# Fused attention and MLP-mixer on one core: the first batch's mask, score tiles and value products regrouped, and its loads issued ahead of the constants

## The chip, the cores and the metric

The kernel runs on 1 core of one Trainium2 chip. The metric is the device time of one execution in microseconds (us); lower is better. Engines are named as in the profile: PE (TensorE matmul), PEld (TensorE weight load), DVE (VectorE), ACT (ScalarE), POOL (GpSimd), SP (SyncE, which here only starts transfers).

## The reference, cut to what matters

```
q, k, v: (8 batches, 8 heads, 576 positions, 64), s: (8, 8, 576)
scores = q @ k^T / 8                        # per batch and head
cum    = cumsum(max(s, 0))
scores = causal ? -1e9 : scores + min(-(cum_i - cum_j), 0)
attn   = softmax(scores)
x      = concat over heads (attn @ v)       # (8, 576, 512)
h      = relu(x^T @ w_tok1) @ w_tok2        # token mixing, 576 -> 256 -> 576
u      = x + h^T
out    = u + relu(u @ w_ch1) @ w_ch2        # channel mixing, 512 -> 1536 -> 512
```

The kernel folds the bias into v: row j of v, and a column of ones beside it, is multiplied by a weight made from exp(cum_j). The product with exp(scores) then gives numerator and denominator together. Only the block diagonal and the block before it are computed (for query block ic, the key blocks ic-1 and ic). A flag, summed at the end, sends the program to a slow general version where this does not hold; with the given inputs it does hold.

## The kernel before, in words

All work is recorded as operations in a `Plan` (helper class at the top). Each operation has an estimated cost per engine that may run it, the things it reads and writes, the ring buffers it holds, and a priority. `Plan.run` is a greedy list scheduler: it puts each operation at its earliest estimated time and so writes a fixed order for each engine. Each engine then runs its list in that order, and a semaphore holds an instruction until what it reads is there. The planner knows nothing of two engines that slow each other, and it fills planned PE gaps in the first 95 us with dummy matmuls on zeros (L947, "fill"), so a PE wait early in the run shows partly as fills. Changing any cost, priority or buffer therefore moves the order of all five lists.

Per batch b (0 to 7) there are four stages.

1. Loads. `stage_qk` (L573) brings k and q of a group of four heads into a `qkn` tile by POOL transfers (L563); a square sum for the flag (L569, ACT) reads the same tiles. `stage_v` (L525) brings v in five chunks of 128 rows (L534: POOL transfers for b = 0 and 1, SP transfers from b = 2), and five multiplies per batch write the weighted copy `vp` (L546; on DVE or POOL for b = 0, on POOL alone after that). The ones column is written by L555 and L557 on POOL. There are two `vf` tiles and two `vp` tiles, one for even and one for odd batches. Eight POOL transfers can be open at a time: a POOL transfer waits for the landing of the eighth before it.
2. Attention. `quad` (L586) turns k and q of four heads with two DVE transposes (L591, into `kT` and `qT`), computes scores on PE (L620) in two column groups (gi = 0 and 1) for two pairs of heads (e = 0 and 1), each into a two-bank PSUM tile `psc` (ring of 2, L415). `soft` takes exp on ACT (L639, 1024 columns) into a ring of four `E` tiles and, for b > 0, multiplies the diagonal blocks by a triangle `keep` on DVE (L647 and L655: the two masks of gi = 1, one of gi = 0). For b = 0 the mask is added on PE instead: an identity matmul of `negm` (L615) ahead of each 128-wide diagonal piece, and the scores are cut into 128-wide pieces to match. `pair` multiplies with `vp` (L677, 9 matmuls a head into one bank `pav`), takes the reciprocal (L684) and writes normalised heads to `x` (L689), one head at a time.
3. Token mixing, `tok` (L724). L742 multiplies x with w_tok1 (two PSUM banks from the ring `pmx`, 3 banks), a relu gives `h` (L752 on ACT or L753 on DVE), L763 multiplies with w_tok2, and the sum with x is made by L766 and L777 (b = 0, PE and ACT) or by a DVE add (L773, into `ub`, `ua` or the shared `us`). The result is transposed: by PE (L799) and a copy (L807, L809) for b = 0 and 1, by an SP transfer (L790) after that.
4. Channel mixing, `chan` (L813). L827 multiplies with w_ch1, L834 (ACT) or L836 (DVE) takes the relu, L845 multiplies with w_ch2, L856 adds and the output leaves by SP (L861, L864).

The order of the weight loads is written by hand at the end (L867 on): after k, q and v of batch 0 come w_tok1 and w_tok2, the four parts of w_ch1, k, q and v of batch 1, and the three parts of w_ch2 (all L699, POOL). A tiny SP transfer (L880, `gate`) waits for the last of these, and the SP loads of v for batch 2 stand behind it.

The start: POOL builds the identity matrices, `keep` and `negm`, and then issues the first loads. The weights `wT` come from s by a chain of ACT, DVE and PE (L484 to L503).

Of the kernel before, what the change touches and what calls it, by code (L numbers as in the profile page):

```python
# [337 lines left out]
def kernel(  # L338
# [12 lines left out]
    nc = tc.nc  # L351
# [30 lines left out]
    negm = sb("negm", [128, 128], BF16, fast)  # L382
# [22 lines left out]
    r_rc = ring("rc", 4, [128, NJ], FP32)  # L405
# [11 lines left out]
    r_mx = ring("pmx", 3, [128, 512], FP32, psum)  # L417
# [14 lines left out]
    nc.vector.memset(zero[:, :], 0.0)  # L432

    def consts():
# [3 lines left out]
    P.op({"POOL": (1.3, 1.5, consts)}, writes=["const"], prio=0)  # L438
    P.op({"POOL": (0.25, 0.45, lambda: nc.gpsimd.tensor_scalar(
        out=negm[:, :], in0=keep[:, :], scalar1=30000.0, scalar2=-30000.0, op0=ALU.mult, op1=ALU.add))},  # L440
        reads=["const"], writes=["negm"], prio=0)
# [38 lines left out]
    def act(n, fn, bias=False):  # L480
# [7 lines left out]
        reads=["sr"], writes=["cum"], prio=-1)  # L488
    P.op(dve(1, lambda: nc.vector.tensor_scalar(
        out=half[:, :], in0=cum[:, S - 1 : S], scalar1=-0.5, scalar2=None, op0=ALU.mult)),  # L490
        reads=["cum"], writes=["half"], prio=-1)
# [3 lines left out]
    bw = Buf(r_mx, False)  # L495

    def w_tr():
        for jc in range(NJ + 1):
            j0 = jc * 128 if jc < NJ else S - 128
            nc.tensor.transpose(out=bw.t[:, jc * 64 : jc * 64 + 64], in_=wn[:, j0 : j0 + 128],  # L500
                                identity=identf[:, :])
    P.op({"PE": (0.7, 1.1, w_tr)}, reads=["wn", "const"], writes=[(bw, 0)], prio=(0,))
    P.op(dve(384, lambda: nc.vector.tensor_copy(  # L503
        out=wT[:, :, :].rearrange("p c e -> p (c e)"), in_=bw.t[:, 0:384])),
        reads=[(bw, 0)], writes=["wT"], prio=-1)
# [17 lines left out]
    vbuf = {}  # L523

    def stage_v(b):  # L525
# [14 lines left out]
        for c in range(NJ):  # L540
# [11 lines left out]
            P.op(alts, reads=[(vf, c), "wT"], writes=[(vp, c)], prio=b * 10 + 5 if b else 0)  # L552
# [32 lines left out]

    def quad(b, qd):  # L586
# [11 lines left out]
        for gi, group in enumerate(([(0, 0, 256), (1, 128, 384)], [(2, 256, 512), (3, 384, 576), (4, 512, 576)])):  # L598
            pss = [Buf(r_sc, False) for e in range(2)]
# [6 lines left out]
            def mm(heads, pss=pss, cols=cols):  # L606
                for (jc, a, z, c0) in cols:
                    j0 = S - 128 if odd and jc == NJ - 1 else jc * 128
                    cuts = sorted({a, min(z, a + 128), z}) if b == 0 else [a, z]
                    for a1, z1 in zip(cuts, cuts[1:]):  # L610
                        o = slice(c0 + a1 - a, c0 + z1 - a)
                        masked = b == 0 and a1 == a
                        if masked:
                            for g in heads:
                                nc.tensor.matmul(out=pss[g // 2].t[:, g % 2, o], lhsT=ident[:, :], rhs=negm[:, 0 : z1 - a1],  # L615
                                                 start=True, stop=False)
                        for e in range(2):
                            for g in heads:
                                rows = slice(32 * g, 32 * g + 32)
                                nc.tensor.matmul(out=pss[g // 2].t[:, g % 2, o], lhsT=kT.t[rows, j0 : j0 + 128, e],  # L620
                                                 rhs=qT.t[rows, a1:z1, e], start=(e == 0 and not masked), stop=(e == 1))
            if b == 0:
                for e in range(2):
                    P.op({"PE": (0.9, 1.2, lambda e=e, mm=mm: mm((2 * e, 2 * e + 1)))},
                         reads=[(kT, 0), (qT, 0), "negm"] + ([("pad", np_ + e)] if 0 < np_ + e < 4 else []),
                         writes=[(pss[e], 0)], holds=[Es[e]], prio=(np_ + e, 1))
            else:
                P.op({"PE": (0.65, 0.95, lambda mm=mm: mm((0, 1, 2, 3)))}, reads=[(kT, 0), (qT, 0)],
                     writes=[(pss[0], 0), (pss[1], 0)], holds=Es, prio=(np_, 1))
            for e in range(2):  # L630
                soft(b, gi, group, pss[e], Es[e])
        for e in range(2):
            pair(b, qd, e, Es[e])

    def soft(b, gi, group, ps, E):
# [4 lines left out]
        P.op(act(1024, ex), reads=[(ps, 0)], writes=[(E, jc) for (jc, a, z) in group], prio=0)  # L640
# [18 lines left out]
    def pair(b, qd, e, E):  # L659
# [8 lines left out]
        for hh in range(2):  # L668
            pa, rc = Buf(r_mx if b == 0 and hh else r_av, False), Buf(r_rc, False)

            def av(pa=pa, hh=hh):
                o = pa.t[:, 0 : NJ * 66].rearrange("p (c n) -> p c n", n=66)
                for ic in range(NJ):
                    j_lo = max(ic - 1, 0)
                    for jc in range(j_lo, ic + 1):
                        d0 = ewin(jc, ic, odd)
                        nc.tensor.matmul(out=o[:, ic, 0 : D + 1], lhsT=E.t[:, hh, d0 : d0 + 128],  # L677
                                         rhs=vp.t[:, jc, h + hh, 0 : D + 1], start=(jc == j_lo), stop=(jc == ic))
            P.op({"PE": (9 * 0.031, 9 * 0.031 + 0.3, av)}, reads=ekeys + vkeys, writes=[(pa, 0)],
                 holds=[x, rc], prio=(np_, 0))  # L680

            def rcp(pa=pa, rc=rc):
                o = pa.t[:, 0 : NJ * 66].rearrange("p (c n) -> p c n", n=66)
                nc.vector.reciprocal(out=rc.t[:, :], in_=o[:, :, D])  # L684
            P.op(dve(30, rcp), reads=[(pa, 0)], writes=[(rc, 0)], prio=0)

            def nrm(pa=pa, rc=rc, hh=hh):
                o = pa.t[:, 0 : NJ * 66].rearrange("p (c n) -> p c n", n=66)
                nc.vector.tensor_tensor(  # L689
                    out=x.t[:, :, (h + hh) * D : (h + hh + 1) * D], in0=o[:, :, 0:D],  # L690
                    in1=rc.t[:, :].unsqueeze(2).to_broadcast([128, NJ, D]), op=ALU.mult)
            P.op(dve(330, nrm), reads=[(pa, 0), (rc, 0)], writes=[(x, h + hh)], prio=0)
# [25 lines left out]
    gate = sb("gate", [1, 16], BF16, fast)  # L718
# [5 lines left out]
    def tok(b):  # L724
# [11 lines left out]
        heads = [(0, 4), (4, 6), (6, H)] if b == 0 else [(0, H)]  # L736
        pms = [Buf(r_mx, False) for t in range(NTC)]
        for (ha, hb) in heads:
            for t in range(NTC):
                def mm(t=t, pm=pms[t], ha=ha, hb=hb):  # L740
                    for c in range(NJ):
                        nc.tensor.matmul(out=pm.t[:, ha * D : hb * D],  # L742
                                         lhsT=w1[:, NJ if odd and c == NJ - 1 else c, t * 128 : t * 128 + 128],
                                         rhs=x.t[:, c, ha * D : hb * D], start=(c == 0), stop=(c == NJ - 1))
                occ = 5 * c_pe((hb - ha) * D)[0]
                P.op({"PE": (occ, occ + 0.3, mm)},
                     reads=[(x, hh) for hh in range(ha, hb)] + ["w1", "padw"],
                     writes=[(pms[t], ha)], holds=[h1], prio=(rank - TOK, 0))
        for t in range(NTC):
            pm = pms[t]  # L750
            P.op(either(512,
# [244 lines left out]
```

## Time and profile before

| what | value |
|---|---|
| three runs | 314.44, 317.94, 314.12 us; median 314.44 |
| profiled execution, its own time | 317.43 us |
| its span in the trace | 315.6 us (1.8 us lie around it) |
| busy in the span | PE 291.2, PEld 166.1, DVE 186.4, ACT 169.8, POOL 80.3 us |
| fills (L947) | 16.0 us of PE's busy time, 7.0 of it before 9.35 us |
| mean clock granted to PE | 0.976 |
| chain that ended last | PE 76%, DVE 11%, DMA 5%, issue 3%, POOL 3% of the span |

The profile cuts the span into 40 slices of 7.9 us and gives the busy tenths of each engine, the clock granted to PE in tenths, and the busy share of the 16 DMA engines. The waits name for each engine what ended its idle time. The timeline lists instructions with start and duration. A line such as L827 is a line of the kernel before.

### The profile page before, as it was taken

The page shows a single profiled execution, that of the slowest core. Times are in us where ns is not written, and L with a number is a line of the kernel's source. Part 1 is how long each engine was busy: PE and PEld are TensorE (multiplying, and loading weights), DVE is VectorE, ACT ScalarE, POOL GpSimd, SP SyncE. Part 2 cuts the span into 40 slices and gives each one's busy share as a digit, 9 for nine tenths or more (in the row PEclk, how much of TensorE's full clock was granted, in tenths as well). Part 3 has the DMA queues.
Part 4 walks back from the last instruction along what each step waited for, and adds up shares of the span by engine and source line. Part 5 has one row for each costly group of instructions (what it writes and reads, how often), then busy time and mean ns, then how long its engine had stood idle before and what let it go on. Part 6 is the DMA issues. An engine that isn't in the chain of part 4 may idle for free.

```text
span 315.6 us, 6588 instructions
## 1 busy us (share of the span) xinstructions
PE 291.2 (92%) x2632; PEld 166.1 (53%) x2663; DVE 186.4 (59%) x391; ACT 169.8 (54%) x274; POOL 80.3 (25%) x123
## 2 busy tenths in 40 slices
PE   7989989992999998999999999996999999999991
PEld 3566875541676544454774545553764545447540
DVE  6843596999599678455744857694615534350020
ACT  3453965883499367621684268873773256107400
POOL 8764660197015212500160101740000000000000
PEclk9999999997599999999999999998999999999999
DMA  5999999999945896916421854499002410051032
GB/s 107 224 206 232 200 210 217 198 258 245 193 77 117 161 134 134 216 40 120 98 39 39 132 140 75 97 139 209 0 2 51 117 66 3 35 122 63 1 105 73
DMA packets 58343, 38.65 MB, mean 122 GB/s; under 512 B 44480, under 2 KB 47936, under 8 KB 58304
## 3 DMA queue, kind: packets, MB, share of 16 engines
q0 software_dynamic: 10128, 17.93, 33.6%
q1 hardware_dynamic: 48176, 20.21, 27.2%
q8 instruction: 23, 0.38, 0.5%
q14 instruction: 16, 0.13, 0.1%
HBM read 40.71 MB, written 9.44 MB: 159 GB/s over the span
## 4 chain that ended last, share of the span: by engine, by line
PE 76%; DVE 11%; DMA 5%; issue 3%; POOL 3%; ACT 0%; SPq 0%; POOLq 0%; DVEq 0%
PE pmx L827 28%; PE pmx L845 26%; PE psc L620 6%; PE pmx L742 5%; PE pav L677 5%; PE pmx L763 4%; DMA uTb<-ub 3%; DVE ub L773 2%; DVE E L647 2%; POOL vp L546 2%; DVE qT L591 2%; DVE kT L591 2%; DVE x L689 2%; DMA qkn<-in_k_dram 1%; PE psc L615 1%
## 5 line engine op out<-in xcount | busy, mean ns | idle before, releaser
L639 ACT ACTIVATE E<-psc 128x1024 bf16<-128x1024 f32 x64 | 62.5, 1024 | 36.6 <-PE psc L620 36.4
L827 PEld LDWEIGHTS <-wc 128*128 128x128 bf16 x624 | 59.6, 99 | 37.0 <-issue 6.1
L827 PE MATMUL pmx<-uTb,wc 128*128 128x320 bf16 x384 | 59.4, 309 | 3.3 <-DMA uTb<-ub 3.1
L845 PE MATMUL pmx<-wc,gb 128*128 128x512 bf16 x231 | 54.0, 379 | 0.5 <-issue 0.2
L834 ACT ACTIVATE gb<-pmx 128x320 bf16<-128x320 f32 x74 | 32.2, 439 | 29.3 <-PE pmx L827 24.3
L569 ACT ACTIVATE junk<-qkn 128x1152 bf16<-128x1152 bf16 x32 | 37.4, 1169 | 14.5 <-DMA qkn<-in_k_dram 8.8
L845 PE MATMUL pmx<-wc,ga 128*128 128x512 bf16 x184 | 44.2, 379 | 0.7 <-DVE ub L773 0.2
L827 PE MATMUL pmx<-uTa,wc 128*128 128x512 bf16 (+1 forms) x237 | 44.4, 336 | 0.2
L546 POOL TENSOR_TENSOR vp<-vf,wT 128x512 bf16<-128x512 f32 (+1 forms) x35 | 37.2, 1082 | 7.5 <-issue 5.1
L845 PEld LDWEIGHTS <-gb 128*128 128x128 bf16 x240 | 22.5, 98 | 25.4 <-issue 0.4
L563 POOL DMA_DIRECT2D qkn<-in_k_dram x20 | 11.2, 562 | 94.0 <-DVE gb L836 22.9
L677 PEld LDWEIGHTS <-E 128*128 128x128 bf16 x576 | 25.7, 98 | 13.5 <-issue 3.7
L834 ACT ACTIVATE ga<-pmx 128x512 bf16<-128x512 f32 (+1 forms) x43 | 21.8, 508 | 20.4 <-PE pmx L827 19.7
L647 DVE TENSOR_TENSOR E<-E,keep 128x512 bf16<-128x512 bf16 x56 | 28.4, 511 | 4.4 <-ACT E L639 4.4
L689 DVE TENSOR_TENSOR x<-pav,rc 128x320 bf16<-128x320 f32 x60 | 29.4, 490 | 1.8
L677 PE MATMUL pav<-vp,E 128*128 128x65 bf16 x540 | 26.7, 194 | 3.7 <-DVE x L689 2.4
L845 PEld LDWEIGHTS <-ga 128*128 128x128 bf16 x192 | 17.7, 98 | 19.8 <-issue 0.7
L684 DVE RECIPROCAL rc<-pav 128x5 f32<-128x5 f32 x60 | 11.2, 187 | 28.3 <-PE pav L677 28.0
L620 PE MATMUL psc<-qT,kT 32*128 32x256 bf16 (+3 forms) x704 | 25.4, 246 | 0.5 <-DVE qT L591 0.2
L763 PE MATMUL pmx<-h,w 128*128 128x512 bf16 x77 | 20.7, 380 | 2.7 <-DVE ub L773 2.6
L591 DVE STREAM_TRANSPOSE kT<-qkn 128x576 f32<-128x576 f32 x16 | 20.0, 1251 | 4.8 <-PE psc L620 3.3
L856 DVE TENSOR_TENSOR of<-pmx,us 128x512 f32<-128x512 f32 x4 | 2.8, 692 | 33.0 <-PE pmx L845 25.1
(84 smaller groups left out, 262.6 us busy)
## 6 DMA issues: line engine op xcount, KB each, us to landing
out_dram<-of SPq DMA_DIRECT2D x32, 256.0 KB, 2.8
vf<-in_v_dram SPq DMA_DIRECT2D x24, 256.0 KB, 5.4
qkn<-in_k_dram POOLq DMA_DIRECT2D x20, 288.0 KB, 5.5
qkn<-in_q_dram POOLq DMA_DIRECT2D x20, 288.0 KB, 6.5
vf<-in_v_dram POOLq DMA_DIRECT2D x8, 256.0 KB, 9.9
wc<-in_moe_w_ch_dram POOLq DMA_DIRECT2D x4, 384.0 KB, 8.8
wc<-in_moe_w_ch_dram POOLq DMA_DIRECT2D x3, 512.0 KB, 11.6
out_dram<-of SPq DMA_DIRECT2D x8, 128.0 KB, 2.4
```

The lines of the kernel that those rows point to most:

```text
L546: eng.tensor_tensor(out=vp.t[p0 : p0 + n, c, :, 0:D], in0=vf.t[p0 : p0 + n, c, :, :], in1=wT[p0 : p0 + n, cw, b * H : b * H + H].unsqueeze ...
L569: P.op({"ACT": (1.2, 1.6, lambda: nc.scalar.activation(out=junk[:, :], in_=n.t[:, :], func=AF.Square, accum_out=sq[:, col : col + 1]))}, r ...
L591: P.op({"DVE": (1.24, 1.4, lambda n=n, dst=dst: nc.vector.transpose(out=dst.t[:, 0:S, :].rearrange("d t e -> d (t e)").bitcast(FP32).rearr ...
L620: nc.tensor.matmul(out=pss[g // 2].t[:, g % 2, o], lhsT=kT.t[rows, j0 : j0 + 128, e], rhs=qT.t[rows, a1:z1, e], start=(e == 0 and not mask ...
L639: nc.scalar.activation(out=E.t[:, :, gi * 512 : gi * 512 + 512], in_=ps.t[:, :, :], func=AF.Exp, scale=0.125)
L647: nc.vector.tensor_tensor(out=o, in0=o, in1=keep[:, :].unsqueeze(1).unsqueeze(1).to_broadcast([128, 2, 2, 128]), op=ALU.mult)
L677: nc.tensor.matmul(out=o[:, ic, 0 : D + 1], lhsT=E.t[:, hh, d0 : d0 + 128], rhs=vp.t[:, jc, h + hh, 0 : D + 1], start=(jc == j_lo), stop=( ...
L689: nc.vector.tensor_tensor(out=x.t[:, :, (h + hh) * D : (h + hh + 1) * D], in0=o[:, :, 0:D], in1=rc.t[:, :].unsqueeze(2).to_broadcast([128, ...
L763: nc.tensor.matmul(out=pm.t[:, :], lhsT=w2[:, t, w0 : w0 + 128], rhs=h1.t[:, t, :], start=(t == 0), stop=(t == NTC - 1 and b > 0))
L827: nc.tensor.matmul(out=pm.t[:, 0 : e - a], lhsT=wc1[:, m, cc * 128 : cc * 128 + 128], rhs=uT.t[:, m, a:e], start=(m == 0), stop=(m == NMC ...
L834: lambda cc=cc, pm=pm, a=a, e=e: nc.scalar.activation(out=g.t[:, cc, a:e], in_=pm.t[:, 0 : e - a], func=AF.Relu),
L845: nc.tensor.matmul(out=pm.t[:, :], lhsT=g.t[:, cc, c * 128 : c * 128 + 128], rhs=wc2[:, cc, :], start=(cc == 0), stop=(cc == NCC - 1))
```

## The change

The first batch is regrouped, and some orders are moved.

- `negm` grows from 128 to 512 columns: zero except three triangles, at columns 0, 256 and 448. For b = 0 one 512-wide identity matmul per head and column group writes the whole bank of mask, and the score matmuls are no longer cut: 256, 192 and 64 columns wide, as for the other batches.
- The three `pmx` banks become one tile, and a `Duo` of two free banks of it serves as a third score tile for b = 0 (two of the eight score tiles).
- For b = 0 the products of two heads go into one two-bank `psc` tile, with one reciprocal and one normalisation per pair.
- The first four loads of k and q are issued on POOL ahead of the constants; the constants and `wT` follow them. `wT` may be copied by ACT.
- `tok` is split by heads for b = 0 (heads 0 to 3 in two `pmx` banks; 4 to 7 in one `psc` tile) and for b = 1 (heads 0 to 3, then 4 to 7).
- The PE transposes of `tok` get a priority between its matmuls, and stores of the output a lower one than other SP work.
- A POOL operation copies one element of each of batch 1's last two `E` tiles into `gate` and is recorded as the writer of "m1", which batch 2's five `vp` multiplies are recorded as reading. Those five are recorded earlier than the writer.

```
-    negm = sb("negm", [128, 128], BF16, fast)
+    negm = sb("negm", [128, 512], BF16, fast)
...
-    r_rc = ring("rc", 4, [128, NJ], FP32)
+    r_rc = ring("rc", 4, [128, 2, NJ], FP32)
...
-    r_mx = ring("pmx", 3, [128, 512], FP32, psum)
+    mxt = psum.tile([128, 3, 512], FP32, name="pmx", tag="pmx")
+    r_mx = Ring("pmx", [mxt[:, i, :] for i in range(3)])
...
+    nc.vector.memset(negm[:, :], 0.0)
...
-    P.op({"POOL": (1.3, 1.5, consts)}, writes=["const"], prio=0)
-    P.op({"POOL": (0.25, 0.45, lambda: nc.gpsimd.tensor_scalar(
-        out=negm[:, :], in0=keep[:, :], scalar1=30000.0, scalar2=-30000.0, op0=ALU.mult, op1=ALU.add))},
-        reads=["const"], writes=["negm"], prio=0)
+    def negs():
+        for a, w in ((0, 128), (256, 128), (448, 64)):
+            nc.gpsimd.tensor_scalar(out=negm[:, a : a + w], in0=keep[:, 0:w], scalar1=30000.0, scalar2=-30000.0,
+                                    op0=ALU.mult, op1=ALU.add)
+    def load_consts():
+        lastp[0] = P.op({"POOL": (1.3, 1.5, consts)}, writes=["const"], prio=0, after=lastp[0])
+        lastp[0] = P.op({"POOL": (0.7, 0.9, negs)}, reads=["const"], writes=["negm"], prio=0, after=lastp[0])
...
-            P.op(alts, reads=[(vf, c), "wT"], writes=[(vp, c)], prio=b * 10 + 5 if b else 0)
+            P.op(alts, reads=[(vf, c), "wT"] + (["m1"] if b == 2 else []), writes=[(vp, c)], prio=b * 10 + 5 if b else 0)
...
+    class Duo:
+        def __init__(self):
+            self.bufs = [Buf(r_mx, False), Buf(r_mx, False)]
+            self.keys = [(x, 0) for x in self.bufs]
+        @property
+        def t(self):
+            lo, hi = sorted(x.slot for x in self.bufs)
+            return mxt[:, lo : hi + 1 : hi - lo, :]
...
-            pss = [Buf(r_sc, False) for e in range(2)]
+            pss = [Duo() if b == 0 and (qd * 4 + gi * 2 + e) % 3 == 2 else Solo(r_sc) for e in range(2)]
...
+                if b == 0:
+                    neg = negm[:, :] if gi else negm[:, 0:256].unsqueeze(1).to_broadcast([128, 2, 256])
+                    for g in heads:
+                        nc.tensor.matmul(out=pss[g // 2].t[:, g % 2, :], lhsT=ident[:, :], rhs=neg, start=True, stop=False)
                 for (jc, a, z, c0) in cols:
                     j0 = S - 128 if odd and jc == NJ - 1 else jc * 128
-                    cuts = sorted({a, min(z, a + 128), z}) if b == 0 else [a, z]
...
+        if b == 1 and qd == 1:
+            P.op({"POOL": (0.15, 0.3, lambda: [nc.gpsimd.tensor_copy(out=gate[0:1, e : e + 1], in_=Es[e].t[0:1, 1, EB[4] : EB[4] + 1])
+                                              for e in range(2)])},
+                 reads=[(Es[0], 4), (Es[1], 4)], writes=["m1"], prio=0)
...
-        for hh in range(2):
-            pa, rc = Buf(r_mx if b == 0 and hh else r_av, False), Buf(r_rc, False)
+        for hs in ([(0, 1)] if b == 0 else [(0,), (1,)]):
+            pa, rc = Solo(r_sc) if b == 0 else Solo(r_av), Buf(r_rc, False)
...
-        heads = [(0, 4), (4, 6), (6, H)] if b == 0 else [(0, H)]
+        cuts = [[(0, 4)], [(4, 6), (6, H)]] if b == 0 else [[(0, 4)], [(4, H)]] if b == 1 else [[(0, H)]]
...
-                 writes=[(pm, 0)], holds=[dst], prio=(rank - TOK, 1))
+                 writes=[(pm, 0)], holds=[dst], prio=(rank - TOK, 1 + 0.1 * c))
...
-            P.op({"PE": (4 * 0.057, 4 * 0.057 + 0.3, tr)}, reads=rk, writes=[(pt, 0)], holds=[uT], prio=(rank - TOK, 2))
+            P.op({"PE": (4 * 0.057, 4 * 0.057 + 0.3, tr)}, reads=rk, writes=[(pt, 0)], holds=[uT], prio=(rank - TOK, 1.15 + 0.1 * c))
...
     stage_qk(0, 0)
     stage_qk(0, 1)
+    load_consts()
+    weights()
     stage_v(0)
```

## The prediction, made before the changed kernel ran

> **What bounds the kernel now.** I read the page's slices first, then PE's waits over the whole span, then windows of the stretch that they point at, then the timelines of POOL and DVE in it.
>
> ```profile
> PE   7989989992999998999999999996999999999991
> PEclk9999999997599999999999999998999999999999
> DMA  5999999999945896916421854499002410051032
> ```
>
> PE is busy nearly throughout; the slices with room are those from 71 to 87 us, where PE falls to 2 and its clock to 7 and 5 tenths, and a small one at 213. The transfer engines are full from 4 us to about 85 us: in that stretch data comes at its own pace, whatever PE does.
>
> ```profile
> PE pmx L799 <- DVE ub L773: 3.6, 1, 3.6
> PE pmx L827 <- DMA uTb<-ub: 3.1, 1, 3.1
> PE pmx L763 <- DVE ub L773: 2.6, 1, 2.6
> PE pav L677 <- POOL vp L546: 1.3, 2, 0.9
> ```
>
> Three of PE's four large waits are for additions and multiplies of other engines. Two (3.6 and 2.6 us) lie in the stretch after 70 us, and one (L677) shows that the products of batch 1 wait for POOL's multiply of v. The 3.1 us at 216 us waits for a transposing transfer of batch 5.
>
> ```profile
> 67.23 4.03 DVE L655 TENSOR_TENSOR E<-E,keep 128x128 bf16<-128x128 bf16 x1
> 67.51 1.05 POOL L546 TENSOR_TENSOR vp<-vf,wT 128x512 bf16<-128x512 f32 x1
> 69.12 2.05 POOL L546 TENSOR_TENSOR vp<-vf,wT 128x512 bf16<-128x512 f32 x2
> 74.04 5.23 POOL L546 TENSOR_TENSOR vp<-vf,wT 128x512 bf16<-128x512 f32 x5
> 74.87 3.50 DVE L647 TENSOR_TENSOR E<-E,keep 128x512 bf16<-128x512 bf16 x1
> ```
>
> Here is the cause. L655 takes 0.21 us elsewhere and L647 0.41 us. Beside POOL's multiplies they take 4.03 and 3.50 us, and the additions for the next stage stand behind them on DVE. These two stalls cost 3.8 and 3.1 us of DVE.
>
> ```profile
> 72.00:76.00 4.00, 1.85 (x16) 1.01 (x17) 4.00 (x6) 1.36 (x2) 2.55 (x3) 0.90 1.15 232
> 76.00:80.00 4.00, 0.98 (x8) 0.85 (x8) 3.97 (x6) 0.42 (x2) 3.19 (x4) 0.50 1.11 233
> 80.00:84.00 4.00, 3.75 (x28) 2.65 (x27) 2.84 (x12) 1.78 (x5) 0.00 (x0) 0.50 1.20 214
> 84.00:88.00 4.00, 4.00 (x40) 2.83 (x39) 1.85 (x4) 2.62 (x5) 0.00 (x0) 0.82 0.63 120
> ```
>
> The columns are PE, PEld, DVE, ACT, POOL busy, the granted clock, transfer share, GB/s. PE loses 6 us of these 16 idle and about 3.3 us more to the half clock. From 88 to 208 us it runs full.
>
> **The change, part by part.** I follow PE past three points that both programs have, by the written instruction orders of the two programs and durations from the timeline.
>
> Loads first. The first load is issued at 2.56 us, behind 1.8 us of constants, and k's first transpose runs at 7.02 us. In the new order it is issued at about 0.75 us, and all first loads come 1.8 us earlier. The constants (1.56 us) and three `negm` pieces (0.29 us or less each) follow four issues (0.72 + 3 x 0.55 us) and end near 5.4 us. `wT` is made from 6.5 us on as before, so they do not bind; v's first three issues move from 4.86 to about 5.5 us, hidden while k and q (four loads at 1.4 us) still use the transfer engines. DVE's new memset (0.27 us, as L432) is long over before the scan at 4.07 us. `wT`'s copy on ACT (0.55 us on DVE) comes ahead of the first exp, where ACT waited 4.5 us.
>
> Score phase of batch 0. Before, ACT's eight exps are 1.44 us apart (10.86 to 20.94), because PE needs two mask groups of 0.28 and two score groups of 0.40 for gi = 0, more for gi = 1, plus fills. Now each tile is two 512-wide mask matmuls (0.21 us each between starts, from L763's 0.43 for two) and eight to twelve score matmuls (0.43, from the 0.57 of sixteen at four heads; I take half the concurrency). That is 0.9 us, and with three tiles ACT's own 1.02 us is the pace. Starting 1.7 us earlier, the exps end at about 17 instead of 21.96 us. Bounds for the mask matmul: 0.21 (L763) to 0.38 us (its unpipelined row); even at 0.38 the pace is 1.2 us.
>
> Products of batch 0. Eight rounds of 0.18 + 0.49 us on DVE become four of about 0.2 + 0.82 (0.49 for 320 columns, 0.69 for 512 in other rows, so 0.82 for 640). The last chunk of v is now multiplied by POOL (1.03 us) instead of DVE (0.69), when it lands near 15.8 us. It ends at 16.9, just ahead of its need. Token mixing then starts near 23.4 us instead of 28.3, and L827 near 28.2 instead of 32.9. So batch 0 gains 4.7 us up to here; w_tok1, w_tok2 and w_ch1 still land first (w_ch1's second part by 23.7 us, read from POOL's eighth-transfer waits).
>
> That POOL multiply has a price: w_tok2's issue, all of w_ch1, k, q and v of batch 1 and w_ch2 stand behind it on POOL. Only the three w_tok1 transfers (1.7 us) are then open. The next data comes about 1.3 us after an issue at 16.9, which leaves a hole of about 0.9 us in a full transfer stream. Bounds: none, if the multiply is over early, to 3.3 us, if the first load's 4.43 us from issue to landing holds on the drained queue. I take 0.9, because the other transfers are still running then. So the stream's lead falls from 1.8 to 0.9 us.
>
> First point, scores of batch 1's second quad (48.95 us). PE's products for batch 1 need POOL's five multiplies, which need v and follow transfers paced by the stream; before, they ended at 43.8. Now 42.9. PE reaches them at about 40.1 us and waits: 3.8 of the 4.7 us are lost here. The next three product rounds alternate with two transposes on DVE as before (0.67 + 1.25 us a round), and PE fills. I get 48.2, at the same work done: a gain of 0.75.
>
> Second point, the end of batch 1's last product (63.1 us). Between them PE is full. Half of batch 1's token mixing (ten 256-wide matmuls, 1.1 us) is moved in here, so I get 63.4.
>
> Third point, batch 1's first L827 (81.09 us, 18.0 after the second). In the new order, counted from 63.4: relus to 3.6, first addition near 4.9 (one mask meets a multiply), a transpose of batch 3's k to 6.9. POOL's last multiply of batch 2 waits for this transpose (the load issued between them reuses its tile). It runs beside two additions, then POOL goes straight on with batch 3's five multiplies (5.2 us). The two gate copies between them (bounds 0.1, POOL's smallest row, to 0.33 us, L555's, each; 0.15 taken) read batch 1's tiles, long finished; two exps of batch 2 wait for them, later than this point. Four masks of DVE (0.41, 0.21, 0.41, 0.21) start exactly there, with two additions, a PE transpose and a copy behind them. With one and a half multiplies waited for by each of the three that collide, masks end at 13.4 and L827 starts at 15.3, that is 78.7 us. The 24 score matmuls that the old order had done by then (0.64) are still to come: a gain of 81.09 - 78.7 - 0.64 = 1.75 us.
>
> Nearest rows for a collision: L647 took 0.56 to 1.17 beside batch 1's multiplies, 3.50 and L655 4.03 beside batch 2's and 3's. Ends: won at every boundary, masks at 11.4 and L827 at 13.1 (gain 3.95); lost at every one, first mask delaying all by 2.5 more, L827 at 19.6 (loss 2.55). The middle is taken because the five collisions of batch 1 each lost about one multiply and the two later ones three or four.
>
> The Trainium skill's page "SBUF — State Buffer", section "Who interferes with whom", says that a VectorE instruction with two SBUF inputs and a GpSimd instruction that reads SBUF take one shared port pair, and that the later one blocks until the first instruction ends. The long rows agree on the blocking but not on its length: L655 sat through three multiplies and a transfer issue. By the rule each mask would wait at most one multiply, and the sum would be the gain of 3.95.
>
> Stores behind other SP work cost nothing: four `of` tiles stand between them and the next add. Afterwards the orders of PE are the same but for details (from batch 3's channel mixing on almost line for line), the clock drop comes again, since PE has little to do for some 5 us, and the 3.1 us of batch 5 stays. I take these at nothing; one 1.4 us wait at 117 us for two products in a row goes, and a run of 40 score matmuls, which must wait for two exps, comes in its place.
>
> Sum: 317.43 - 1.75 = 315.7 for the profiled execution. It stands 3.0 above the median of 314.44, about what one more lost stall costs; I carry the difference to the median: **312.7 us**.
>
> **Rivals.**
> - *The cover goes.* If DVE's masks run before POOL's batch 3 multiplies, L827 starts at 63.4 + 10.6 = 74.0, a gain of 6.45, and the 3.6 us of half clock go too: 304.4. For it: the new order has additions ahead of scores. Against: the two streams start within 0.7 us of each other.
> - *The early gain survives.* If v of batch 1 is multiplied by 40.1 instead of 42.9, 2.8 us more are kept: 309.9. Against: the transfer row reads 9 throughout.
> - *DVE loses every boundary.* As worked out above, L827 at 83.0: 314.44 + 2.55 = 317.0, slower than before. It decides once L827 starts later than 80.45 us. For it: the 4.03 us row. Against: batch 1's rows.
> - *The hole in the stream is 3.3 us.* Then the lead of 0.9 becomes a lag of 1.5, and 312.7 + 2.4 = 315.1. Against: 4.43 us was on an empty queue, and here three transfers still move.
>
> **How the numbers follow.** Mine 0.58, cover gone 0.12, early gain kept 0.10, every boundary lost 0.14, hole 0.06. My own case spans 310.5 to 315. The range leaves out the deeper half of the first rival and the end of the third with its clock: 306.5 to 317.5. About 2% is what a measurement of this kernel can tell from no change, that is 308.15 and 320.7. Faster: the first rival and a little of the second and of mine, 0.14. Slower: only a lost clock on top of the third, 0.04. The same: 0.82.
>
> **What would show it.** Right: exps of batch 0 about 1.05 us apart and over by 17.5; L877 of batch 0 (L827 before) from 28 us; PE idle or filling near 41 to 43 with POOL's multiply as releaser; masks of several us beside POOL's multiplies between 66 and 78 us, clock near 0.5 after them. Wrong: batch 1's products not waiting for POOL, masks at 0.4 us throughout, no clock drop near 75 us (then it is far faster), or w_tok2 landing after 24 us.

## The result, and the profile after

The changed kernel takes 497.06 us (median of four runs, 493.8 to 506.97) against 314.35 us for the kernel before, measured beside it: a ratio of 1.574, 95% interval 1.558 to 1.589. The forecast was 312.7 us in a range of 306.5 to 317.5. The profiled execution took 497.43 us, with a span of 495.6 us and a granted clock of 0.938.

PE's slices and its clock, on the page of the changed kernel:

```profile
PE   7985669766767676776676877676667767665583
PEclk9998589988999989999959999999999999799788
```

PE's row had a 9 in nearly every slice; now hardly a slice reaches 9, from the first to the last. So this is no stall in one place. PE's waits over the span (what PE waited with, for whom: us in total, times, longest us) say for whom:

```profile
PE pmx L877 <- ACT gb L884: 32.4, 60, 1.5
PE pmx L877 <- ACT ga L884: 20.0, 34, 1.1
PE pmx L895 <- DVE of L906: 13.3, 19, 0.8
PE pmx L877 <- DVE gb L886: 9.7, 14, 1.2
PE pmx L877 <- DVE ga L886: 7.8, 11, 0.9
PE pmx L813 <- DVE ub L823: 7.7, 6, 3.2
```

Before, all of PE's waits together came to 16.3 us in 19 waits; now they come to 141.4 us in 213 waits. 120 us of them have an operation that empties a `pmx` bank as their releaser: the relus L884 and L886, the additions L906 and L823. PE's busy time grew too, from 291.2 to 347.6 us. 125.1 us more of waits and 56.4 us more of busy time are 181.5 us; the spans differ by 180.0.

One stretch of channel mixing shows the pattern, first of the kernel before, then of the changed kernel (start, duration, engine and operation; the bracket is the idle time before and its releaser):

```profile
155.07 2.34 PE L827 MATMUL pmx<-uTb,wc 128*128 128x320 bf16 x16
155.81 1.52 ACT L834 ACTIVATE gb<-pmx 128x320 bf16<-128x320 f32 x3 [0.38 <-PE pmx L827]
```

```profile
241.17 0.44 ACT L884 ACTIVATE gb<-pmx 128x320 bf16<-128x320 f32 x1 [2.26 <-PE pmx L877]
...
241.66 0.70 PE L877 MATMUL pmx<-uTb,wc 128*128 128x320 bf16 x4 [0.25 <-ACT gb L884]
...
242.40 0.44 ACT L884 ACTIVATE gb<-pmx 128x320 bf16<-128x320 f32 x1 [0.79 <-PE pmx L877]
242.88 0.70 PE L877 MATMUL pmx<-uTb,wc 128*128 128x320 bf16 x4 [0.53 <-ACT gb L884]
...
```

Before, PE runs 16 matmuls, four groups, in one piece (0.585 us a group), while ACT empties the banks of the groups ahead. After, PE does four matmuls (0.70 us), ACT takes the relu (0.44), and only then PE does the next four: 1.22 us a group, although two of the three banks are free all the time. The relu starts as soon as the group ends and PE starts as soon as the relu ends, so the two engines take turns.

### The profile page after: what moved, and what is told of

Read it like the earlier page. It is cut to its first block, busy times and chain, and to the rows that moved or that the text cites. A ratio compares the mean times of both kernels' runs of the same rounds, so it can differ in the third digit from the quotient of the medians.

```text
span 495.6 us, 6478 instructions
## 1 busy us (share of the span) xinstructions
PE 347.6 (70%) x2592; PEld 174.4 (35%) x2592; DVE 187.7 (38%) x383; ACT 171.6 (35%) x278; POOL 82.5 (17%) x128
## 4 chain that ended last, share of the span: by engine, by line
PE 62%; DVE 18%; ACT 14%; issue 4%; DMA 1%; ACTq 0%; DVEq 0%
PE pmx L877 25%; PE pmx L895 21%; ACT gb L884 6%; DVE of L906 4%; ACT ga L884 4%; PE pmx L813 4%; PE pmx L787 4%; PE psc L647 2%; DVE ub L823 2%; DVE gb L886 2%; DVE E L679 2%; DVE ga L886 2%; DVE ua L823 1%; PE pmx L999 1%; PE pav L715 1%
## 5 line engine op out<-in xcount | busy, mean ns | idle before, releaser
L877 PEld LDWEIGHTS <-wc 128*128 128x128 bf16 x624 | 63.4, 102 | 126.5 <-issue 97.9
L877 PE MATMUL pmx<-uTb,wc 128*128 128x320 bf16 x384 | 69.5, 310 | 44.2 <-ACT gb L884 32.4
L671 ACT ACTIVATE E<-psc 128x1024 bf16<-128x1024 f32 x62 | 60.4, 1024 | 58.1 <-PE psc L647 58.1
L877 PE MATMUL pmx<-uTa,wc 128*128 128x512 bf16 (+1 forms) x240 | 55.7, 367 | 29.4 <-ACT ga L884 20.0
L895 PE MATMUL pmx<-wc,gb 128*128 128x512 bf16 x240 | 60.8, 397 | 16.5 <-DVE of L906 8.6
L884 ACT ACTIVATE gb<-pmx 128x320 bf16<-128x320 f32 x76 | 32.6, 437 | 102.9 <-PE pmx L877 93.2
L895 PE MATMUL pmx<-wc,ga 128*128 128x512 bf16 x192 | 49.5, 394 | 16.7 <-DVE of L906 4.7
L884 ACT ACTIVATE ga<-pmx 128x512 bf16<-128x512 f32 (+1 forms) x46 | 23.2, 513 | 74.0 <-PE pmx L877 50.7
L895 PEld LDWEIGHTS <-gb 128*128 128x128 bf16 x240 | 23.7, 101 | 47.5 <-issue 26.3
L813 PE MATMUL pmx<-h,w 128*128 128x512 bf16 x80 | 23.1, 386 | 17.1 <-DVE ub L823 7.7
L895 PEld LDWEIGHTS <-ga 128*128 128x128 bf16 x192 | 18.9, 100 | 41.2 <-issue 25.4
L906 DVE TENSOR_TENSOR of<-pmx,us 128x512 f32<-128x512 f32 x4 | 2.8, 692 | 73.6 <-PE pmx L895 37.3
L647 PE MATMUL psc<-qT,kT 32*128 32x256 bf16 (+1 forms) x620 | 24.8, 265 | 1.8 <-ACT E L671 1.7
L886 DVE TENSOR_SCALAR ga<-pmx 128x512 bf16<-128x512 f32 (+1 forms) x14 | 8.1, 577 | 43.4 <-PE pmx L877 34.2
L906 DVE TENSOR_TENSOR of<-pmx,ua 128x512 f32<-128x512 f32 x16 | 11.1, 691 | 35.1 <-PE pmx L813 14.8
```

The lines of the kernel that those rows point to most:

```text
L671: nc.scalar.activation(out=E.t[:, :, gi * 512 : gi * 512 + 512], in_=ps.t[:, :, :], func=AF.Exp, scale=0.125)
L813: nc.tensor.matmul(out=pm.t[:, :], lhsT=w2[:, t, w0 : w0 + 128], rhs=h1.t[:, t, :], start=(t == 0), stop=(t == NTC - 1 and b > 0))
L877: nc.tensor.matmul(out=pm.t[:, 0 : e - a], lhsT=wc1[:, m, cc * 128 : cc * 128 + 128], rhs=uT.t[:, m, a:e], start=(m == 0), stop=(m == NMC ...
L884: lambda cc=cc, pm=pm, a=a, e=e: nc.scalar.activation(out=g.t[:, cc, a:e], in_=pm.t[:, 0 : e - a], func=AF.Relu),
L886: lambda cc=cc, pm=pm, a=a, e=e: nc.vector.tensor_scalar_max(out=g.t[:, cc, a:e], in0=pm.t[:, 0 : e - a], scalar1=0.0)),
L895: nc.tensor.matmul(out=pm.t[:, :], lhsT=g.t[:, cc, c * 128 : c * 128 + 128], rhs=wc2[:, cc, :], start=(cc == 0), stop=(cc == NCC - 1))
```

## The experiments

The theory after this reading: the waits go by the tile and not by the bank. With three tiles a group waits for the last reader of its own bank; with one tile it waits for the last reader of any of them, and the relu waits for the newest group in any of them. Rivals: the regrouped order and the longer waits of the first batch cost the time, or the lower clock does.

**One tile on the kernel before.** Lines, the number of banks and the order of the instructions on each engine are those of the kernel before.

```
-    r_mx = ring("pmx", 3, [128, 512], FP32, psum)
+    mxt = psum.tile([128, 3, 512], FP32, name="pmx", tag="pmx"); r_mx = Ring("pmx", [mxt[:, i, :] for i in range(3)])
```

> The kernel before with one edit: the three pmx banks are declared as one tile of 3 x 512 and the ring hands out its slices; banks, instructions and their order on each engine stay as they were. Theory (waits go by the whole tile: a relu waits for the newest matmul group written anywhere in it, a matmul group for the newest relu that read anywhere in it, so that PE and ACT/DVE take turns): 475 to 505 us, nearly all of the 183 us, with PE's matmuls at L827 and L845 waiting for ga, gb and L856 at hundreds of places and the granted clock near 0.94. Rival (the regrouped order, the shared score banks or the longer waits of the first batch cost it): 312 to 318 us. Rival (the lower clock alone): 314 us, since nothing here asks for less clock.

Measured: 500.4 us, ratio 1.584 (1.575 to 1.593). PE's waits in this run:

```profile
PE pmx L827 <- ACT gb L834: 34.5, 65, 1.5
PE pmx L827 <- ACT ga L834: 18.6, 30, 1.8
PE pmx L845 <- DVE of L856: 14.0, 19, 1.0
```

They are the waits of the changed kernel, with nothing else of the change in place. This declaration alone costs the whole difference. It adds up in the same way: waits 16.3 to 149.8 us, busy time 291.2 to 340.1, together 182.4 us for 182.2 us of span. The clock rival falls. Nothing here asked for less clock, and the mean did come to 0.918, but the turn-taking runs at full clock too. PE's rows in 40 slices of 12.4 us:

```profile
PE   7865768937676756676568767756677766766683
PEclk9987699978999999999999999999999998755588
```

From the 11th slice to the 33rd the clock row reads 9, while PE is busy 5 to 7 tenths, with one 8. The low clock, mostly in the last slices, is a part of the 48.9 us of longer busy time, not the cause.

**Two banks in one tile, the third by itself.**

```
+    mxt, mx2 = psum.tile([128, 2, 512], ...), psum.tile([128, 512], ...)
+    r_mx = Ring("pmx", [mxt[:, 0, :], mxt[:, 1, :], mx2[:, :]])
```

> The kernel before with two of the three pmx banks as one tile and the third as a tile of its own. Theory (waits by tile): a group in the tile's second bank lets the relu of its first bank wait, but the group in the third bank runs meanwhile, so most of the turn-taking is covered: 320 to 390 us, well below half of the loss of the single tile. Rival (a cost per access to a wider tile, or per slice): about two thirds of the whole loss, 430 us. Rival (the tile has nothing to do with it): 314 us.

Measured: 354.66 us, ratio 1.126 (1.120 to 1.132), a fifth of the loss. PE's largest wait in it, and a stretch of its channel mixing:

```profile
PE pmx L827 <- ACT gb L834: 6.6, 16, 1.1
```

```profile
318.27 1.79 PE L827 MATMUL pmx<-uTb,wc 128*128 128x320 bf16 x12 [0.37 <-ACT gb L834]
...
320.43 1.79 PE L827 MATMUL pmx<-uTb,wc 128*128 128x320 bf16 x12 [0.37 <-ACT gb L834]
```

PE now does three groups in one piece and then waits 0.37 us: 0.72 us a group, where one tile has 1.22 and three tiles 0.585. All its waits come to 45.7 us in 80 waits. The rival with a price per access to a slice had 430 us and falls; what counts is whether work in another tile lies between.

**The change with three tiles.** The third score tile is then two tiles, read by two 512-wide exps. A second version leaves it out and uses `psc` alone for batch 0's scores.

```
-    mxt = psum.tile([128, 3, 512], FP32, name="pmx", tag="pmx")
-    r_mx = Ring("pmx", [mxt[:, i, :] for i in range(3)])
+    r_mx = ring("pmx", 3, [128, 512], FP32, psum)
...
# second version, besides:
-            pss = [Duo() if b == 0 and (qd * 4 + gi * 2 + e) % 3 == 2 else Solo(r_sc) for e in range(2)]
+            pss = [Solo(r_sc) for e in range(2)]
```

> The changed kernel with its three pmx banks as three tiles again; a score tile of two of them is read by two 512-wide exps in place of one of 1024 (two such score tiles in batch 0, about 0.2 us more of ACT each). Everything else of the change stays. Theory (only the single tile was left out of my sum): the rest of my sum holds, 306.5 to 317.5 us, 313 the likeliest; batch 0's channel mixing starts near 28 us. Rival (the regrouping of the first batch or the order costs the 183 us): above 450 us.

> The changed kernel with three pmx tiles and batch 0's scores in the two psc tiles only, so the exps are single again and wait for two tiles in turn. Theory: as with three tiles, the pace of the exps a little longer (1.2 to 1.4 us for 1.05), hidden behind v of batch 1: 307 to 318 us, within 1.5 us of the other. Rival (the third score tile carries the gain): 2 us or more slower than the other.

Measured: 323.33 us, ratio 1.024 (1.020 to 1.029), and 323.93 us, ratio 1.024 (1.018 to 1.029). So 173 of the 183 us are back, and the third score tile gains nothing. But the rest of the sum is wrong as well: it said 312.7, and the kernel without the single tile is 2.4% slower than before, outside the range. PE's waits in the second version:

```profile
PE pav L715 <- POOL vp L555: 4.9, 5, 1.4
PE pav L715 <- DVE E L679: 4.4, 1, 4.4
...
PE pmx L849 <- DVE ub L823: 2.3, 1, 2.3
PE psc L647 <- ACT E L671: 2.2, 3, 1.1
```

The first line is batch 1's products waiting for v, the second a mask beside POOL's multiplies. Four runs took these apart.

**Where batch 0's and batch 1's v are multiplied.** With three tiles and no third score tile: batch 0 on DVE alone (first), batch 1 on DVE and batch 0's last chunk on POOL as in the change (second), both on DVE (third).

```
-            if b == 0:
-                alts["DVE"] = (0.76, 0.98, lambda mul=mul: mul(nc.vector))
+            if b == 0:      # third run: b <= 1
+                alts = {"DVE": (0.76, 0.98, lambda mul=mul: mul(nc.vector))}
...
# second run:
+            if b <= 1:
+                alts = {**(alts if b == 0 else {}), "DVE": (0.76, 0.98, lambda mul=mul: mul(nc.vector))}
```

> Against the changed kernel with three separate tiles and no third score tile (323.9 us, L877 of batch 1 from 84.99 us): the last chunk of batch 0's v is multiplied by DVE again, so no POOL multiply stands ahead of the loads. Theory hole (the transfer stream stood nearly empty from 16 to 18.8 us, where my sum had 0.9 us): transfer share about 1.1 at 16 to 20 us, batch 1's v multiplied by about 43.3 in place of 46.0 us, 320 to 321.5 us. Theory collisions (what is missing is DVE masks that sit through whole runs of POOL multiplies): the masks still take 4 to 5 us, 322.5 to 325.

> The same kernel with three tiles, but batch 1's five multiplies of v on DVE (0.69 us each) in place of POOL (1.04); batch 0's last chunk stays on POOL. Theory collisions: the mask of 5.06 us at 40 us shrinks to 0.4, batch 1's second scores come 3 to 4 us earlier than 52.5 us, 319 to 321 us. Theory hole: v lands as late as before this edit, so the products still wait for it, and the five multiplies are 3.5 us more of DVE: 322.5 to 325.

> Both edits together: batch 0's last chunk and batch 1's five on DVE. If hole and collision are two causes in a row, they add: 315 to 318.5 us. If one hides the other, no better than the better of the two alone, 319 to 321.

Measured: 324.62 us, ratio 1.027 (1.021 to 1.032); 311.6 us, ratio 0.989 (0.984 to 0.995); 307.46 us, ratio 0.974 (0.969 to 0.978). The hole by itself gives nothing: v of batch 1 comes 2.0 us earlier, but PE's waits for the addition L823 grow from 2.3 to 5.5 us, 2.1 of them behind small operations of the flag (of which more below). Batch 1's multiplies give more than either theory said, and then the hole shows another 4 us. The third of these is 2.6% faster than the kernel before. PE's largest wait in it:

```profile
PE pmx L877 <- DMA uTb<-ub: 4.2, 1, 4.2
```

No other is above 1.2 us: PE waits 0.3 us for POOL, and for no mask, although one mask still takes 4.07 us (at 86.44 us). But this edit also makes the planner lay the order anew, so it does not tell waits from masks.

**Early loads alone.** The kernel before, with its constants and the making of `wT` moved behind the first four loads, all of batch 0's v on DVE:

```
     stage_qk(0, 1)
+    load_consts()
+    weights()
     stage_v(0)
```

> The kernel before with one part of the change alone: the first four loads are issued ahead of the constants, masks 128 wide as before, all of batch 0's v on DVE. My sum's theory (the transfers set the pace up to 85 us, so what starts 1.8 us earlier comes 1.8 us earlier, unless a mask meets a run of POOL multiplies): 312 to 314 us. Rival (the early gain is lost at the waits for batch 1's v and at the masks): 314 to 318.

Measured: 316.17 us, ratio 1.001 (0.998 to 1.004). My sum's theory missed; the rival held. The two masks that sit beside POOL's multiplies are there again, of 4.02 and 3.50 us, only 2.3 us later in the run.

**Multiplies of v in other combinations.** The kernel before with batch 1 on DVE (`b <= 1` as above); the fastest version with the third score tile; the fastest version with batch 2 on DVE too (`b <= 2`); and the changed kernel, single tile and all, with `b <= 1`.

> The kernel before with batch 1's multiplies of v on DVE and nothing of the change. If the gain of 16 us against the three-tile kernel is only that DVE's masks no longer meet runs of POOL multiplies, the kernel before gains as much as its own stalls are worth (1.3 us of PE waiting for POOL at the products, some of the 6.2 us at the additions): 307 to 311 us. If the change's early loads, 512-wide masks and paired heads carry the gain once no mask is hit: 312 to 317 us.

> The fastest version so far (three tiles, batch 0's last chunk and batch 1's five on DVE, 307.5 us) with the third score tile over two pmx tiles put back (two 512-wide exps for it). Theory (batch 0 is then ahead of its data anyway): 306 to 309 us. Rival (the exps' pace sets the end of batch 0 now that the hole and the collision are gone): 305 us or less.

> The fastest version so far with batch 2's five multiplies on DVE too. Theory collisions: two masks of batch 1 take 1.36 and 0.94 us beside batch 2's multiplies in that version, so little is left to gain, and five times 0.69 us come on a DVE that is over 9 tenths busy there: 307 to 312 us. Rival (every POOL multiply beside masks costs): 304 to 306 us.

> The changed kernel as it is, with the single pmx tile, and the same two edits to v's multiplies. Theory (the waits of the single tile are on PE's path at nearly every matmul group): the 16 us do not come off, since DVE and POOL have room there: 488 to 498 us. Rival (the two losses add): 478 to 483 us.

Measured: 318.16 us, ratio 1.007 (1.003 to 1.011), slower than either theory had it, since PE now waits 6.5 us for an addition near 78 us (see below); 313.04 us, ratio 0.986 (0.979 to 0.992), so the third score tile costs here; 307.99 us, ratio 0.970 (0.963 to 0.977), not to be told from the fastest version; 490.94 us, ratio 1.552 (1.539 to 1.565): in the changed kernel as it stands the edit gives little, and PE's largest wait there is still the one for the relu L884 (32.1 us in 60 waits).

The addition of the first of these runs does not stand behind a mask, but behind a small copy that belongs to the flag. It runs beside a row of five POOL multiplies; in the kernel before it takes 0.16 us:

```profile
73.25 4.40 DVE L905 COPY bad<-gap 64x4 f32<-64x4 f32 x1
```

**Masks without a second operand.** Each mask multiply from batch 1 on becomes a memset of the same block on DVE, so those scores are not masked; the order on every engine and the waits stay. On the change with three tiles, on the kernel before, on the version with batch 0's v on DVE, and on the fastest version:

```
-            nc.vector.tensor_tensor(out=o, in0=o, in1=keep[:, :]..., op=ALU.mult)
+            nc.vector.memset(o, 0.5)
```

> The changed kernel with three tiles (323.9 us), every mask multiply of DVE from batch 1 on replaced by a memset of the same block to 0.5 (so the scores are not masked there); order and waits unchanged. Theory collisions (a DVE operation with two SBUF operands sits through a run of POOL multiplies): memsets take 0.2 to 0.5 us everywhere, batch 1's L877 starts near 78 to 80 us for 84.99, 313 to 317 us. Rival (the planner's order is the cause): 321 us or more.

> The kernel before with the same replacement. Theory collisions: its two stalls of 4.03 and 3.50 us go, and with them the additions behind them come 3 to 6 us earlier and the half clock near 75 us mostly goes: 305 to 311 us. Rival (PE's waits there have another cause): 314 to 317 us.

> The three-tile kernel with batch 0's last chunk of v on DVE (324.6 us) and the same replacement: hole and collisions both gone, batch 1's v still on POOL. Theory: with the masks out of the way the 2 to 3 us of the hole show, 2 to 3 us below the run with the hole: 311 to 314 us. Rival (the hole is hidden either way): within 1 us of it.

> The fastest version (307.5 us, v of batches 0 and 1 on DVE) with the same replacement, as a control: its masks meet no run of multiplies that PE waits for, so the replacement by itself, about 0.1 us less per mask, should give 305 to 307.5 us. If it falls below 303, the shorter DVE work counts by itself and the other three runs have to be read with that taken off.

Measured: 314.69 us, ratio 0.999 (0.995 to 1.002); 307.36 us, ratio 0.974 (0.970 to 0.979); 316.9 us, ratio 1.005 (1.001 to 1.009); 302.03 us, ratio 0.955 (0.950 to 0.960). The first two came out as the theory of collisions had them. The third did not: closing the hole with the masks out costs 2.2 us, where 2 to 3 us less were expected. There the flag's small operations meet POOL's multiplies in the masks' place: three two-operand ones (L954) take 3.85 us, 0.28 in the kernel before, and the copy 1.03. PE waits 4.1 us for the addition behind them. The control fell by 5.4 us, below its bound, so whole times mislead here. The start of the first L895 (L845 before) of each batch, read from the timelines, tells where each gain arises:

| kernel (us) | batch 0 | 1 | 2 | 3 | 4 | 5 | 6 | 7 |
|---|---|---|---|---|---|---|---|---|
| before | 47.72 | 102.76 | 136.17 | 167.28 | 198.08 | 237.15 | 267.54 | 296.11 |
| change, one tile | 78.11 | 150.27 | 203.87 | 261.16 | 306.92 | 364.60 | 410.21 | 469.87 |
| change, three tiles, no third score tile | 51.26 | 106.32 | 141.54 | 174.29 | 205.56 | 244.38 | 274.94 | 303.18 |
| the same, memset | 51.40 | 99.39 | 132.92 | 166.46 | 197.69 | 233.77 | 264.33 | 292.57 |
| before, memset | 47.83 | 94.68 | 128.38 | 159.66 | 190.84 | 226.09 | 256.48 | 285.04 |
| fastest | 44.00 | 89.08 | 122.52 | 155.73 | 187.78 | 228.12 | 258.68 | 286.92 |
| fastest, memset | 45.55 | 89.54 | 122.98 | 156.31 | 188.11 | 224.35 | 254.91 | 283.16 |

Up to batch 1 the memset takes 6.9 us off the change, 8.1 off the kernel before and nothing off the fastest version. Another 2.7 to 4.1 us go at batch 5 in all three, where PE waits for a transposing transfer. So up to batch 1 the masks that meet POOL's multiplies are worth about 7 us in the change and 8 in the kernel before, and the change did not make them dearer. With the masks out of the way the change still stands behind the kernel before: by 3.6 us at batch 0 and 7.5 at batch 7. That part is neither tile nor mask, though not free of collisions: in the memset run of the change PE still waits 1.6 us behind the flag's operations.

It begins where batch 1's products wait. Windows of the change with three tiles and no third score tile (PE, PEld, DVE, ACT, POOL busy, clock, transfer share, GB/s), then of the kernel before:

```profile
40.00:42.00 2.00, 0.34 (x4) 0.12 (x2) 2.00 (x2) 0.47 (x2) 1.99 (x5) 1.00 1.22 201
42.00:44.00 2.00, 0.38 (x4) 0.27 (x4) 2.00 (x1) 0.00 (x0) 2.00 (x3) 0.60 1.25 209
44.00:46.00 2.00, 0.42 (x4) 0.20 (x3) 2.00 (x2) 0.00 (x0) 1.92 (x2) 0.50 1.24 205
46.00:48.00 2.00, 1.92 (x10) 1.37 (x10) 1.74 (x4) 0.38 (x1) 0.02 (x1) 0.50 1.22 213
```

```profile
42.00:44.00 2.00, 0.70 (x12) 0.56 (x11) 2.00 (x3) 0.41 (x2) 1.75 (x2) 1.00 1.26 209
44.00:46.00 2.00, 2.00 (x27) 1.81 (x26) 1.97 (x6) 1.15 (x3) 0.00 (x0) 1.00 1.15 210
```

PE comes to the products just after 40 us and does two of them after each of POOL's multiplies until 46 us; this adds up to the 4.9 us of the first line of its waits, and with the masks out it is still 4.7. Then its clock is 0.50, so that the 12 matmuls behind take 2.74 us, where the kernel before has 1.47. The kernel before waits 1.3 us for POOL here, and its clock stays at 1.00.

Why v is late shows in the windows of the same version at 16 us, and on POOL there:

```profile
16.00:18.00 2.00, 1.85 (x23) 1.01 (x24) 0.00 (x0) 1.52 (x3) 2.00 (x3) 1.00 0.10 17
18.00:20.00 2.00, 1.71 (x40) 1.48 (x40) 1.02 (x3) 0.93 (x1) 2.00 (x4) 1.00 0.75 104
```

```profile
15.89 1.04 POOL L555 TENSOR_TENSOR vp<-vf,wT 64x512 bf16<-64x512 f32 x1 [2.34 <-DMA vf<-in_v_dram]
16.88 0.78 POOL L735 DMA_DIRECT2D w<-in_moe_w_tok_dram  x1
```

The transfers behind the multiply are issued from 16.88 us on, after the queue has run dry. Against a share of 1.15, as in the windows behind them, the two windows lack an estimated 2.5 us of transfers (2 x 1.05 and 2 x 0.40, over 1.15). That is the hole. Closing it brought v of batch 1 from 46.0 to 44.0 us.

## Why the prediction was wrong, point by point

- **The failed step** is the sentence "Afterwards the orders of PE are the same but for details … I take these at nothing". It is true of the orders and false of the waits. The lines of the diff that make three `pmx` banks one tile have no term in my sum: I took them for another way of naming the same banks. They cost 182 us of span by themselves, as the first experiment shows: PE waits for a relu or an addition at most groups. No rival held it either; that a wait might be added at every group was never asked.

The other points are read in the version with three tiles and no third score tile (323.93 us), where the turn-taking does not cover them. L877 of batch 1 began there at 84.99 us, 6.3 us later than forecast, and another 3.4 us were lost after it; most of the 11 us above the forecast of 312.7 lie in the terms below.

- **Loads first, score phase.** The first load was issued at 1.23 us (0.75 forecast, 2.56 before), and the first exp began 1.6 us earlier (1.7 forecast). The constants ended at 6.6 us, not 5.4, so v's first issues came at 6.58, not 5.5. The exps' pace was 1.26 us with two score tiles, where I had 1.05 with three, and they ended at 18.9 us instead of about 17. L877 of batch 0 began at 29.2 us (28.2 forecast, 32.9 before), so batch 0 gained 3.7 of the 4.7 us. In the changed kernel itself it began at 43.7.
- **The hole.** Taken at 0.9 us, about 2.5 by the estimate above: it lies within the bound of 3.3, but the choice within it was too small. v of batch 1 was multiplied by 46.0 us, not 42.9. Even with the hole closed it was 44.0 us, against 43.8 in the kernel before, so the lead of 1.8 us that I set against the hole was gone as well: POOL's issues of w_tok1 began at 11.70 us in that version (11.09 before), and its transfers from 16 to 20 us moved 143 GB/s for 201.
- **First point.** 48.2 us forecast, 52.5 measured. 3.1 us of it are v. The half clock after PE's stand, 1.3 us on one run of matmuls, had no term, though I priced it at 72 us. The wait itself and its place were right.
- **Second point.** 63.4 forecast, 67.1 measured: the same lag, carried along.
- **Third point.** 15.3 us after the second forecast, 17.9 measured. The masks met the multiplies, as foreseen, but lost more than the one and a half I allowed. One of them before the first point (40.07 us, beside batch 1's multiplies) and one after the second are these:

```profile
40.07 5.06 DVE L679 TENSOR_TENSOR E<-E,keep 128x512 bf16<-128x512 bf16 x1
...
76.69 5.66 DVE L679 TENSOR_TENSOR E<-E,keep 128x512 bf16<-128x512 bf16 x1
```

  The rivals "DVE loses every boundary" and "the hole" therefore both came true in part in the version with three tiles, with the clock on top: 17.9 us lies between my 15.3 and the 19.6 of every boundary lost, and 2.5 us between my 0.9 and 3.3. I had given each its chance as if only one could.
- **Afterwards.** The run of score matmuls that has to wait for two exps, which I had set against a wait that goes, cost more than it: at 122 us PE waits 1.75 us for exps and then runs at a clock of 0.57. By the table, another 3.4 us are lost between batch 1 and batch 3 (from 3.6 to 7.0 behind the kernel before).

```profile
122.17 0.29 PE L647 MATMUL psc<-qT,kT 32*128 32x256 bf16 x2 [1.12 <-ACT E L671]
123.09 0.63 PE L647 MATMUL psc<-qT,kT 32*128 32x256 bf16 x14 [0.63 <-ACT E L671]
...
124.15 4.22 PE L895 MATMUL pmx<-wc,gb 128*128 128x512 bf16 x11
```

  Eleven matmuls take 4.22 us here; the kernel before has eleven in 2.54.

- **Two readings.** The four windows from 72 to 88 us show 5.4 us without PE's work, not 6. The half clock there is put at 3.3 us in one place and at 3.6 in the rival "the cover goes". Neither enters the sum that gives 312.7.

What stays open: which of the change's parts carries the gain of the fastest version. The early loads alone gave nothing, the multiplies on DVE alone cost 0.7%, and mask, paired heads and split token mixing were not tried apart. Why one mask sits through one multiply and another through five was not settled either.

## What to carry to other kernels

Compare what each instruction waits for, not only the order of the instructions: buffers that an engine fills while others empty them must be tiles of their own, or the engines take turns. An edit that looks like a declaration gets a term in the sum like any other, and the trace of before gives its bounds: here a group of 0.585 us and a relu of 0.44 us that either overlap or take turns, and PE's waits went from 19 to 213. A start that comes earlier is worth only what the next transfer-paced wait leaves of it, and if PE stands there it pays the clock on top.

## What the runs showed of the hardware

- A DVE multiply with two SBUF operands sat through up to five POOL multiplies (5.06 and 5.66 us for 0.41). Beside another run of them a copy of 64 x 4 elements took 4.40 us for 0.16. The Trainium skill's page "SBUF — State Buffer", section "Who interferes with whom", calls the shared port pair an exclusive lock; these runs agree that one engine stands while the other works, and show that the waiting engine may not get its turn between two multiplies. A memset of the same block in the same place and order was not held up:

```profile
40.28 0.48 DVE L679 MEMSET E<- 128x512 bf16 x1
```

- PE's clock fell to 0.50 although PE was not wholly idle: it did two small matmuls every 1.0 to 1.6 us from 41 to 46 us. In the first experiment, with a wait at most groups but PE busy for 68.7 us of the 100 from 300 to 400 us, it stayed at 1.00.
- A group of four 320-wide matmuls takes 0.70 us by itself and 0.585 us in a run, so waits between groups lengthen PE's busy time as well.
- The Trainium skill's page "PSUM — Partial Sum Buffer", section "PSUM bank collisions raise a hardware error", gives the rule to guard PSUM by bank and quadrant. The runs show the price of guarding more than that at once: 1.58 times the time for three banks together, 1.13 for two of three.
